# Longer planned latencies for three DMA steps in the scheduler of the second MoE

## The chip, the cores and the metric

One Trainium2 chip, one NeuronCore. The metric is the device time of one execution in microseconds (us). TensorE (PE) multiplies matrices, VectorE (DVE) and ScalarE (ACT) work elementwise, GpSimd (POOL) does little here, and SyncE (SP) issues every DMA of the part that matters. Each engine runs its own instructions in the order in which the program gives them; a later one can't pass an earlier one that still waits.

## The reference, cut to what matters

Three layers follow one another in fp32: an attention with pooled keys and values, a first MoE with ELU, and a second MoE (its weights are dense) on 4608 tokens of 512 values. Only the second is touched:

```
h = x @ w_in                                  # 4608x512 @ 512x1024
e = exp(h - max(h));  sm = e / (sum(e) + 1e-9)
solu = h * sm
ln = (solu - mean(solu)) / sqrt(var(solu) + 1e-6) * g_ln
out = ln @ w_out                              # 4608x1024 @ 1024x512
```

## The kernel before, in words

Every fp32 product is made of three products of rounded halves (high by high, low by high, high by low). So each operand has a high part, copied by ACT, and a low part, which DVE makes by subtraction.

The second MoE runs from about 877 us to the end. Its 4608 tokens are 18 pairs of tiles, each tile of 128 tokens. For pair `n` the first product is a seven-product scheme of Strassen's kind. PE makes `P1`, `P2`, `S2`, `S1`, `S3`, `T4`, `S4` (each six matmuls of 512 columns, line 1015) in three PSUM banks X, Y, Z. Between them ACT copies a bank's intermediate state to SBUF (`snap`, line 1025, tile `sn`): PE may not go on in that bank until the copy is done. After `P1`, for instance, PE makes `P2` in another bank, and then `S2` must wait for the snap of X.

The tile that becomes complete with `T4` is called A here (its values are in `hb`), the one complete with `S4` is B (in `ha`). Each then takes the same chain, with these names in the planner: `max` (DVE, line 1066), `exp` (ACT, 1072), `mul` (DVE, 1078), `sub` (ACT, 1083), `sq` (ACT, 1088), `var`. The result has to be transposed for the second product. For the 16 middle pairs, 32 tiles, that goes through DRAM: DVE transposes blocks of 32x32 (`T`, 1102), SP stores the tile to `zd` (`s`, 1107, one DMA of 512 KB), SP loads it back in four DMAs of 128 KB into `dT` (`l`, 1114). SP can't issue `l` before the store has landed. Then ACT makes the high part (`hi2`, 1122), DVE the low part (`lo2`, 1126), and PE the second product (`po`, 1153, 24 matmuls). ACT scales it into `ot` (`st`, 1159) and SP stores that to the output (1160). `os` stands for the landing of that store; the next `st` has one buffer and needs it. The first and the last pair are transposed on PE instead and have no `s` or `l`.

The order of PE's work is written out by hand (`seq`): per pair five products, `po` of B of the pair before last, `T4`, `S4`, `po` of A of the last pair. The order of ACT, DVE and SP comes from `arrange`, a list scheduler that runs when the kernel is built. Every step is an `op` with an engine, a duration, the steps that it depends on, and `lat`, the time after its end until its result may be used. From these `arrange` works out, backward, the latest start of each step at which PE's hand-written order still keeps its times, and, forward, when each becomes ready. It hands each engine the ready step with the earliest latest start, with small corrections for waits:

```python
x = min([latest[q] for q in after[k]], default=t + 3.0) - o["dur"] - o["lat"] - (gap if o["eng"] else 0.0)
latest[k] = min(x, want.get(k, x))
...
done[k] = start + o["dur"] + o["lat"]
...
(k for k in c if ready[k] <= first + look), key=lambda k: latest[k] + 3.0 * max(0.0, ready[k] - first)
```

with `gap = 0.06` and `look = 0.35`. Steps are then written to the program in the order of their planned starts. Waits in the program are set by data dependencies alone: the planned times are in no instruction.

Of the kernel before, what the change touches and what calls it, by code (L numbers as in the profile page):

```python
# [20 lines left out]
def kernel(  # L21
# [80 lines left out]
    st = {}  # L102
# [1350 lines left out]
    for pr in range(NTP):  # L1453
# [54 lines left out]
        for s in range(7):  # L1508
            banks = o_banks(s)
            for t in range(4):  # L1510
                mul_o(s, t, banks, s in (0, 1, 2), s in (1, 5, 6))
                if s + 1 < 7:
                    for i in range(2):
                        w_ring(("o", s + 1, 2 * t + i))
                    n = ORDER[s + 1]
# [47 lines left out]
    def tiles_of(n):  # L1563

        c, q = divmod(n, 2)
        return 4 * c + q + 2, 4 * c + q
# [87 lines left out]
    tiles = [i for n in range(NPAIR) for i in tiles_of(n)]  # L1654
    outs = [i for key, i in seq if key == "po"]

    def op(key, eng, dur, deps, f=None, *a, lat=0.0, at=0.0):
        ops[key] = dict(eng=eng, dur=dur, deps=deps, lat=lat, at=at, f=f, a=a)
# [3 lines left out]
    for key, n in seq:  # L1662
        k = (key, n)
        if key == "po":
            j = outs.index(n)
# [17 lines left out]
    for n, (a, b) in enumerate(map(tiles_of, range(NPAIR))):  # L1683
        if n > 1:
            c = n // 2
            if n % 2 == 0 and c > 1:
                old = [(k, 2 * c - 3) for k in ("sums", "h0", "hi", "l0", "lo")] if c > 2 else []
                op(("xl", c), "SP", 0.55, old, p2_load, c, lat=5.0, at=20.0 if c == 2 else 0.0)
            x = [("xl", c) if c > 1 else "x1", ("S4", n - 2)]
            op(("open", n), None, 0.0, x, p2_open, n)  # L1690
            op(("sums", n), "DVE", 1.45, [("open", n), ("lo", n - 2), ("hi", n - 2)], p2_sums, n)
            op(("h0", n), "ACT", 0.95, [("open", n)], p2_hi, n, slice(0, 2))
            op(("hi", n), "ACT", 1.02, [("sums", n)], p2_hi, n, slice(2, 3))
            op(("l0", n), "DVE", 1.0, [("h0", n)], p2_lo, n, slice(0, 2))
            op(("lo", n), "DVE", 1.18, [("hi", n)], p2_lo, n, slice(2, 3))
        ha = ("s" if n > 2 else "sub", B_(max(n - 2, 0)) if n > 1 else None)
        hb = ("s" if n > 2 else "mul", A_(n - 1) if n > 2 else A_(0) if n == 2 else None)
        op(("p1", n), "ACT", 0.56, [("P1", n), ("ha0", n - 1)], snap, n, "p1", "X")
        op(("u2", n), "ACT", 0.56, [("S2", n), ("hb1", n - 1)], snap, n, "u2", "X")
        op(("u3", n), "ACT", 0.56, [("S3", n), ("ha0", n), ("ha1", n - 1)], snap, n, "u3", "X")  # L1700
        op(("ha0", n), "DVE", 0.62, [("P2", n), ("p1", n), ha], z_add, n, "ha0")
        op(("hb1", n), "DVE", 0.66, [("S1", n), ("u3", n), hb], z_add, n, "hb1")
        op(("hb0", n), "ACT", 0.57, [("T4", n), ("hb1", n)], z_add, n, "hb0")
        op(("ha1", n), "DVE", 0.66, [("S4", n), ("u2", n), ("ha0", n)], z_add, n, "ha1")
        for i, h, key in ((a, ("hb0", n), "b"), (b, ("ha1", n), "a")):
            j, jo = tiles.index(i), outs.index(i)
            e2 = [(k, tiles[j - 2]) for k in ("T", "pe", "sq")] if j > 1 else []
            op(("max", i), "DVE", 1.18, [h, ("hb1", n)] + ([("st", tiles[j - 6])] if j > 5 else []), s_max, i, n, key)
            op(("exp", i), "ACT", 1.3, [("max", i)] + e2, s_exp, i)
            op(("mul", i), "DVE", 1.75, [("exp", i)], s_mul, i)  # L1710
            op(("sub", i), "ACT", 1.12, [("mul", i)], s_sub, i)
            op(("sq", i), "ACT", 1.2, [("sub", i)], s_sq, i)
            op(("var", i), "DVE", 0.12, [("sq", i)], s_var, i, lat=0.9)
            free3 = [("po", outs[jo - 3])] if jo > 2 else []
            if n in (0, last):
                op(("hi2", i), "ACT", 1.08, [("pe", i)] + free3, t_ph, i)
                op(("lo2", i), "DVE", 1.3, [("hi2", i)], t_pl, i)
            else:
                op(("T", i), "DVE", 1.18, [("sub", i)], t_dve, i)
                op(("s", i), "SP", 0.4, [("T", i)], t_store, i, lat=2.4)  # L1720
                op(("l", i), "SP", 1.75, [("s", i)] + ([("lo2", tiles[j - 2])] if n > 1 else []), t_load, i, lat=2.1)
                op(("hi2", i), "ACT", 1.0, [("l", i)] + free3, t_hi, i)
                op(("lo2", i), "DVE", 1.2, [("hi2", i)], t_lo, i)
            op(("st", i), "ACT", 0.66, [("po", i), ("var", i)] + ([("os", outs[jo - 1])] if jo else []), z_store, i)
            op(("os", i), None, 0.0, [("st", i)], lat=2.4)
    for o in ops.values():
        o["deps"] = [d for d in o["deps"] if d in ops]
    with tc.manual_schedule():
# [38 lines left out]
```

## Time and profile before

| what | value |
|---|---|
| median of three runs | 1273.57 us (1273.32 to 1275.31) |
| the profiled execution | 1271.55 us, of which its span 1269.4 us |
| granted clock of TensorE over the span | 0.993 of full speed |
| PE busy | 1242.0 us, 98% |
| DVE busy | 984.8 us, 78% |
| ACT busy | 824.0 us, 65% |
| from 870 us to the end: PE, DVE, ACT busy | 387.70, 285.60, 254.30 us |

A span runs from the first to the last instruction; a time is somewhat longer. Starts are counted from the span's start. A row of waits names the engine that stood idle and, after the arrow, what released it; PEld is PE's loading of weights, SPq the queue of SP. A granted clock of 1.00 is 2.4 GHz.

### The profile page before, as it was taken

The numbers are of one execution on the slowest core, as the hardware profiler recorded it, in microseconds if no ns is written. First come the engines' busy times: TensorE is split into PE (matmuls) and PEld (weight loads), VectorE is DVE, ScalarE is ACT, GpSimd is POOL, SyncE is SP. The second block draws the span as 40 slices with busy tenths as digits, with TensorE's granted clock in tenths as the row PEclk, the third lists the DMA queues.
The fourth block names the chain that finished last, engine by engine and source line by source line (L and its number), as shares of the span: only waits on it lengthen the run. The fifth ranks groups of instructions, "written<-read, shape, count | busy, mean of one in ns | idle before, by whom it ended". The sixth has DMA issues, their size and how long they took to land.

```text
span 1269.4 us, 17238 instructions
## 1 busy us (share of the span) xinstructions
PE 1242.0 (98%) x5768; PEld 993.9 (78%) x5768; DVE 984.8 (78%) x1484; ACT 824.0 (65%) x1405; POOL 177.7 (14%) x148
## 2 busy tenths in 40 slices
PE   8899999999999999999999999999998999999998
PEld 6777877777777878778888778888886878887777
DVE  8898687978877799676795778986886777778673
ACT  7887566666757784457764468743776667667564
POOL 4564222333210000100000000000000000000000
PEclk8999999999999999999999999999998999999999
DMA  9975366675768867787666888878454544544341
GB/s 323 296 218 191 125 220 221 214 234 168 237 205 274 252 214 243 222 294 199 203 215 201 287 254 270 288 256 306 151 172 141 158 140 143 169 147 141 108 143 57
DMA packets 177065, 263.30 MB, mean 207 GB/s; under 512 B 16465, under 2 KB 96849, under 8 KB 175953
## 3 DMA queue, kind: packets, MB, share of 16 engines
q1 hardware_dynamic: 176976, 262.21, 64.5%
q8 instruction: 46, 0.75, 0.2%
q14 instruction: 43, 0.34, 0.1%
HBM read 182.46 MB, written 79.69 MB: 207 GB/s over the span
## 4 chain that ended last, share of the span: by engine, by line
PE 64%; DVE 13%; DMA 13%; ACT 5%; issue 2%; SPq 2%; POOL 0%; ACTq 0%; DVEq 0%; POOLq 0%
PE hA L818 12%; PE oA L908 11%; PE o L694 9%; PE h L639 9%; PE po L1153 5%; DMA dT<-zd 4%; PE at L192 3%; PE oB L908 3%; PE zX L1015 3%; DMA zd<-ha 2%; PE at L277 2%; PE pt L251 2%; PE hB L818 2%; SPq L1114 2%; DVE e L1078 2%
## 5 line engine op out<-in xcount | busy, mean ns | idle before, releaser
L1153 PE MATMUL po<-w,dhl 128*128 128x512 f32 x864 | 203.7, 392 | 0.0
L908 PE MATMUL oA<-op,wr 128*128 128x512 f32 x864 | 202.4, 392 | 0.0
L908 PEld LDWEIGHTS oA<-op,wr 128*128 128x128 f32 x864 | 160.8, 188 | 38.1 <-issue 2.9
L1153 PEld LDWEIGHTS po<-w,dhl 128*128 128x128 f32 x864 | 162.1, 188 | 35.3
L898 ACT CAST op<-g 128x1024 fp32r<-128x1024 f32 x84 | 87.9, 1050 | 72.3 <-PE oA L908 33.3
L899 DVE TENSOR_TENSOR op<-g,op 128x1024 fp32r<-128x1024 f32 x84 | 102.8, 1230 | 34.1 <-ACT op L898 33.8
L818 PE MATMUL hA<-sS,wr 128*128 128x512 f32 x432 | 108.8, 394 | 1.5 <-ACT sp L830 1.5
L1015 PE MATMUL zX<-w,xh 128*128 128x512 f32 x288 | 102.8, 398 | 7.5 <-ACT sn L1025 7.4
L1093 POOL TENSOR_TENSOR sc<-sc,mhalf 128x1 f32<-128x1 f32 x36 | 21.1, 595 | 575.1 <-DVE sc L1092 300.1
L560 POOL TENSOR_TENSOR wol<-wo,woh 128x512 fp32r<-128x512 f32 x48 | 74.0, 1543 | 172.7 <-ACT woh L559 172.7
L818 PEld LDWEIGHTS hA<-sS,wr 128*128 128x128 f32 x432 | 79.9, 188 | 21.1 <-ACT sp L830 3.0
L241 POOL TENSOR_TENSOR es<-es,sm 128x720 f32<-128x720 f32 x28 | 48.2, 1720 | 305.7 <-DVE sm L239 137.3
L639 PE MATMUL h<-xh,wh 128*128 128x512 f32 x192 | 79.6, 415 | 2.4 <-DVE e L656 2.4
L694 PE MATMUL o<-gh,woh 128*128 128x512 f32 x192 | 77.5, 404 | 0.0
L838 DVE SCALAR_TENSOR_TENSOR g<-ep,g 128x512 f32<-128x512 f32 x72 | 50.9, 712 | 33.9 <-ACT ep L837 33.6
L639 PE MATMUL h<-xh,wl 128*128 128x512 f32 x192 | 76.2, 397 | 0.0
L639 PE MATMUL h<-xl,wh 128*128 128x512 f32 x192 | 76.0, 396 | 0.0
L694 PE MATMUL o<-gh,wol 128*128 128x512 f32 x192 | 75.1, 391 | 0.0
L1126 DVE TENSOR_TENSOR dhl<-dT,dhl 128x1024 fp32r<-128x1024 f32 x32 | 39.2, 1225 | 44.0 <-ACT dhl L1122 43.9
L1015 PEld LDWEIGHTS zX<-w,xh 128*128 128x128 f32 x288 | 54.7, 190 | 23.3 <-ACT sn L1025 11.0
L1122 ACT CAST dhl<-dT 128x1024 fp32r<-128x1024 f32 x32 | 33.6, 1049 | 46.9 <-DMA dT<-zd 46.8
L836 ACT ACTIVATE ep<-g 128x512 f32<-128x512 f32 x72 | 44.9, 628 | 26.2 <-DVE g L870 13.3
(354 smaller groups left out, 2759.8 us busy)
## 6 DMA issues: line engine op xcount, KB each, us to landing
wr<-w1d SPq DMA_DIRECT2D x168, 256.0 KB, 3.9
wr<-w3d SPq DMA_DIRECT2D x168, 256.0 KB, 3.0
raw<-in_w SPq DMA_DIRECT2D x48, 512.0 KB, 5.6
dT<-zd SPq DMA_DIRECT2D x128, 128.0 KB, 2.8
v<-in_v SPq DMA_DIRECT2D x32, 288.0 KB
x1r<-x1d SPq DMA_DIRECT2D x9, 1024.0 KB, 16.1
out<-ot SPq DMA_DIRECT2D x36, 256.0 KB, 3.7
w1d<-ci SPq DMA_DIRECT2D x16, 512.0 KB, 2.9
```

What stands on the lines that cost most here:

```text
L241: eng.tensor_tensor(es, es, bc(sm, n), op=ALU.mult)
L560: nc.gpsimd.tensor_tensor(ol, t[:, f % 4, :], oh.bitcast(F32), op=ALU.subtract)
L639: nc.tensor.matmul(h[:, 0:n], a[g][:, kk, fo:fo + P], x[j][:, kk, 0:n], start=(kk == 0 and m == 0), stop=(kk == KDM - 1 and m == 2), skip_ ...
L694: nc.tensor.matmul(acc, a[:, dm * P:(dm + 1) * P], x[:, 0:n], start=(f == 0 and m == 0), stop=(f == NF - 1 and m == 2))
L818: nc.tensor.matmul(bank, w[:, a, kk], x[:, b, kk], start=(start and m == 0), stop=(stop and m == 5), skip_group_check=True,)
L836: nc.scalar.activation(e, h, AF.Relu, scale=-1.0)
L838: gate["dve"] = nc.vector.scalar_tensor_tensor(d, e, 1.0, h, op0=ALU.subtract, op1=ALU.max).ins
L898: gate["act"] = nc.scalar.copy(o[:, 0], src).ins
L899: gate["dve"] = nc.vector.tensor_tensor(o[:, 1], src, o[:, 0].bitcast(F32), op=ALU.subtract).ins
L908: nc.tensor.matmul(banks[d], ws[i][:, a, d * P:(d + 1) * P], o[:, b, i], start=(start and t == 0 and i == 0 and m == 0), stop=(stop and t ...
L1015: nc.tensor.matmul(bank, x[:, o:o + P], w[:, y + k, :], start=(start and m == 0), stop=(stop and m == 5), skip_group_check=True,)
L1153: nc.tensor.matmul(po, a[:, c], b[c // 4][:, c % 4, :], start=(m == 0), stop=(m == 3 * NC2 - 1))
```

## The change

Three numbers of the plan change. The landing of the store `s` is counted at 3.0 us in place of 2.4, that of the loads `l` at 4.0 in place of 2.1, and that of the output store `os` at 3.5 in place of 2.4. No instruction is added or removed, and PE's order stays; what can differ is the order of the steps on ACT, DVE and SP (and the issue of POOL's small steps, which go with `var`).

```diff
                 op(("T", i), "DVE", 1.18, [("sub", i)], t_dve, i)
-                op(("s", i), "SP", 0.4, [("T", i)], t_store, i, lat=2.4)
-                op(("l", i), "SP", 1.75, [("s", i)] + ([("lo2", tiles[j - 2])] if n > 1 else []), t_load, i, lat=2.1)
+                op(("s", i), "SP", 0.4, [("T", i)], t_store, i, lat=3.0)
+                op(("l", i), "SP", 1.75, [("s", i)] + ([("lo2", tiles[j - 2])] if n > 1 else []), t_load, i, lat=4.0)
                 op(("hi2", i), "ACT", 1.0, [("l", i)] + free3, t_hi, i)
                 op(("lo2", i), "DVE", 1.2, [("hi2", i)], t_lo, i)
             op(("st", i), "ACT", 0.66, [("po", i), ("var", i)] + ([("os", outs[jo - 1])] if jo else []), z_store, i)
-            op(("os", i), None, 0.0, [("st", i)], lat=2.4)
+            op(("os", i), None, 0.0, [("st", i)], lat=3.5)
```

## Rows read from the trace of the kernel before

**Rows 1.** Waits of PE's matmuls, 870 us on: waiter, releaser, total us, times, longest.

```profile
PE zX L1015 <- ACT sn L1025: 7.4, 6, 4.1
```

**Rows 2.** Busy time of a stretch: length, then PE, PEld, DVE, ACT, POOL, clock, DMA.

```profile
960.00:980.00 20.00, 15.88 (x59) 12.44 (x58) 13.09 (x26) 12.04 (x19) 1.61 (x3) 0.83 0.62 183
```

**Rows 3.** Waits of all engines, 870 us on.

```profile
ACT dhl L1122 <- DMA dT<-zd: 46.8, 28, 4.2
```

**Rows 4.** Timeline of ACT around 970 us: start, length, idle before with its releaser.

```profile
969.69 1.04 ACT L1122 CAST dhl<-dT 128x1024 fp32r<-128x1024 f32 x1 [4.17 <-DMA dT<-zd]
970.64 1.14 ACT L1083 ACTIVATE e<-e,sc 128x1024 f32<-128x1024 f32 x1
971.82 1.06 ACT L1088 ACTIVATE sq<-e 128x1024 bf16<-128x1024 f32 x1
...
972.88 0.57 ACT L1025 COPY sn<-zX 128x512 f32<-128x512 f32 x1
```

**Rows 5.** Timeline of PE at the same place.

```profile
973.50 0.79 PE L1015 MATMUL zX<-w,xh 128*128 128x512 f32 x1 [4.12 <-ACT sn L1025]
```

**Rows 6.** Chain of waits that ended last, its pieces there: start, us, what.

```profile
973.50 2.93 PE zX L1015 x6
976.42 2.56 PE zZ L1015 x6
978.98 1.39 PE zX L1015 x6
980.37 5.49 PE po L1153 x24
```

**Rows 7.** Timelines of DVE and SP: the tile of rows 4, its transposition and DMAs.

```profile
958.76 1.24 DVE L1102 STREAM_TRANSPOSE ha<-e 128x1024 f32<-128x1024 f32 x1
...
960.02 0.38 SPq L1107 DMA_DIRECT2D zd<-ha  x1
960.46 0.54 SPq L958 DMA_DIRECT2D x1r<-x1d  x1
963.29 1.74 SPq L1114 DMA_DIRECT2D dT<-zd  x4
```

**Rows 8.** Timelines of DVE, SP and ACT: `T`, `s`, `hi2` of the tile with the longest way.

```profile
1189.54 1.24 DVE L1102 STREAM_TRANSPOSE ha<-e 128x1024 f32<-128x1024 f32 x1
...
1192.84 1.27 SPq L1107 DMA_DIRECT2D zd<-ha  x1
...
1201.38 1.05 ACT L1122 CAST dhl<-dT 128x1024 fp32r<-128x1024 f32 x1 [2.56 <-DMA dT<-zd]
```

**Rows 9.** Query of the tile `dT`, 880 us on: issue to landing of one quarter.

```profile
DMA to landing us min/median/max: 2.2/2.8/5.3
```

**Rows 10.** Timelines of DVE and PE: `T`, `lo2`, `po` of the first tile A.

```profile
907.20 1.23 DVE L1102 STREAM_TRANSPOSE hb<-e 128x1024 f32<-128x1024 f32 x1
...
916.75 1.22 DVE L1126 TENSOR_TENSOR dhl<-dT,dhl 128x1024 fp32r<-128x1024 f32 x1 [0.62 <-ACT dhl L1122]
...
919.58 0.62 PE L1153 MATMUL po<-w,dhl 128*128 128x512 f32 x2
```

**Rows 11.** The same three for the tightest tile A, the fourteenth of sixteen.

```profile
1186.88 1.23 DVE L1102 STREAM_TRANSPOSE hb<-e 128x1024 f32<-128x1024 f32 x1
...
1197.07 1.23 DVE L1126 TENSOR_TENSOR dhl<-dT,dhl 128x1024 fp32r<-128x1024 f32 x1 [2.51 <-ACT dhl L1122]
...
1199.39 0.85 PE L1153 MATMUL po<-w,dhl 128*128 128x512 f32 x3
```

**Rows 12.** The same three for the last tile A.

```profile
1226.50 1.25 DVE L1102 STREAM_TRANSPOSE hb<-e 128x1024 f32<-128x1024 f32 x1
...
1235.98 1.22 DVE L1126 TENSOR_TENSOR dhl<-dT,dhl 128x1024 fp32r<-128x1024 f32 x1 [1.17 <-ACT dhl L1122]
...
1241.51 0.85 PE L1153 MATMUL po<-w,dhl 128*128 128x512 f32 x3
```

**Rows 13.** Waits of SP's queue, 880 us on.

```profile
SPq L1160 <- ACT ot L1159: 100.8, 30, 10.7
```

## The prediction

> **What bounds the kernel now.** The page says that PE is busy for 98% of the span, so a gain can come only from the little that PE loses. Which part of that lies in the second MoE is read from the waits of PE from 870 us on: six waits of 7.4 us in sum, all of them for a snap (line 1025) [rows 1]. The longest is 4.1 us. The busy time by stretch shows that it cost more than its length: from 960 to 980 us the granted clock is 0.83 [rows 2], so part of that stretch ran at 1.2 GHz. The chain of waits gives the size: the two products behind the gap took 2.93 and 2.56 us, the next one 1.39 [rows 6], so (2.93 - 1.39) + (2.56 - 1.39) = 2.7 us. PE's loss here that any order could give back is 7.4 + 2.7 = 10.1 us.
>
> Next, why a snap is late. At the long gap, PE's wait in bank X ended at 973.50 with a snap [rows 5] that ACT began only at 972.88 [rows 4]. In front of it ACT stood idle for 4.17 us with `hi2` at its head, waiting for a load, and then ran `hi2`, `sub` and `sq` before the snap. Nothing of these three is needed by `S2`. And the tile was in no hurry: `hi2` ended at 970.73 and `lo2` takes 1.22 us [rows 10], so it was ready near 972.0, while its `po` began at 980.37 [rows 6]. It is a tile B. All six gaps have this form: a `hi2` of a tile B that waited between 1.5 and 4.2 us and then a late snap; the first is that of rows 4, the last that of rows 8.
>
> The waits of all engines say how common the cause is: ACT waited for the loads at 28 of 32 `hi2`, 46.8 us in sum [rows 3]. Mostly PE had enough in hand; six times not.
>
> **Why the plan puts `hi2` too early.** From the end of `T` to the earliest `hi2` the old plan counts 0.06 + 0.4 + 2.4 + 0.06 + 1.75 + 2.1 + 0.06 = 6.83 us, so 6.83 + 1.0 + 0.06 = 7.89 to the earliest `lo2`. In the trace, `lo2` begins 8.3 us after the end of `T` for the first tile A, 9.0 for the fourteenth, 8.2 for the last [rows 10 to 12]. For the B of rows 4, `hi2` began 9.69 us after `T` ended at 960.00 [rows 4, 7]; a load of x went out on the same queue between its store and its loads [rows 7]. The longest way of all 32 is 1201.38 - 1190.78 = 10.60 us [rows 8]. So the old plan is too short nearly always, by 0.1 to 3.8 us, and ACT meets `hi2` before its data.
>
> **The change, part by part.** Nothing is added or removed; the work of each engine stays. Two things happen in the planner.
>
> First, `hi2` can't be planned before 6.83 + (3.0 - 2.4) + (4.0 - 2.1) = 9.33 us after `T`. In ACT's order it moves behind what becomes ready in those 2.5 us: at the gap of rows 4 that is `sub` (1.14 us), `sq` (1.06) and the snap (0.57), which is the right cure. ACT will then wait only for loads that take longer. Of the 32, six did so, by 3.3 us in sum; the longest is 10.60 - 9.33 = 1.27 us [rows 8], the B of rows 4 has 9.69 - 9.33 = 0.36. So of 46.8 us of waiting some 3.3 remain. What remains of PE's gaps lies between nothing and these 3.3; four of the six are among the tiles for which a wait remains. Gaps have been shorter than the waits behind them (7.4 against 46.8 in all, 4.12 against 4.17 at worst), so I take 0.8. The clock's loss goes with the long gap. This term is 10.1 - 0.8 = 9.3 us of gain, between 0 (other steps come to stand in front of the snaps in the same way) and 10.1.
>
> Second, all that leads to `T` becomes due 2.5 us earlier, and tiles A lose room. From the end of `T` to the start of `po` they had 11.15, 11.28 and 13.76 us in rows 10, 11 and 12; 11.15 is the least and 12.97 the mean of the sixteen. The new plan wants 9.33 + 1.0 + 0.06 + 1.2 = 11.59. If `T` stays where it is, three of sixteen miss that, by 0.4, 0.3 and less than 0.1 us: 0.8 us of PE waiting for `lo2`. If moreover one more step of 1.15 us falls in front of `hi2` or `lo2`, the need is 12.74, seven of sixteen miss it, and the sum is 6.3 us. If `T` is planned earlier, as its earlier due time makes likely where DVE has a choice, the loss is nothing. I take 0.8, the value without any further accident, and keep 0 and 6.3.
>
> An earlier due time for A has its own price: `max`, `exp`, `mul` and `sub` of A now win against other steps more often, and on ACT these are the snaps. A snap takes 0.57 us [rows 4] and PE has 1.39 us of work in the other bank [rows 6]: 0.8 us to spare. An `exp` or `sub` of 1.15 us begun just before a snap is ready holds PE for 0.35 us; `sub` and `sq` together, 2.4 us with the accumulator's read, for 1.6. The trace of before has such a queue only behind a wait, so the bounds are 0 and, once in each of 16 pairs at the higher price, 26. The planner compares due times and a snap's is within 0.8 us of its ready time, while A keeps some of its room; so I take three cases at 0.35, about 1.0 us.
>
> B's room is no concern (8.4 us in the case above, and 2.5 are taken). The landing of `os` matters to `st` alone: outputs come 8.2 or more us apart (`po`, 5.49, with 2.7 us of products between), and 0.66 + 3.5 is less, so this edit costs nothing; at the end, with two `po` in a row, 5.49 still covers it. On SP, `l` is planned 0.6 us later and may fall behind an output store, whose wait for `st` is up to 10.7 us [rows 13]. Today's case of this kind is the 2.0 us for which the `s` of rows 8 was held, behind loads that waited for their own store. The plan's later `l` lets such an `s` go ahead and may hold another `l`; I set both against each other, at nothing, with 2.0 us of a tile's room as the bound, which B's room covers.
>
> Sum: -9.3 + 0.8 + 1.0 = -7.5 us. The profiled execution took 1271.55 us, so it would take 1264.05; the median of the runs is 2.0 us higher, and the gain taken from it gives 1266.1.
>
> The Trainium skill says otherwise (DMA: Bandwidth & Descriptors, Anatomy of one DMA): it counts about 2.0 us and the bytes at 436 GB/s, which makes an estimate of 2.3 us for a quarter of 128 KB. That is for DMAs issued by GpSimd; by it the old 2.1 is about right, the new 4.0 is 1.7 us too long, and the tiles are held back for nothing. The trace's median is 2.8, its longest 5.3 [rows 9].
>
> **The rivals.** *The plan now holds back tiles whose data is there.* Typical A tiles had `lo2` 8.2 to 9.0 us after `T` and the plan now says 10.39, so 1.4 to 2.2 us are given away. For it: A's least room. Against it: even then only three miss. With one more step in front, PE loses 6.3 us at `po`, the gain is 9.3 - 6.3 = 3.0, and the time 1270.5. It cancels the gain where the delay beyond the plan reaches 1.5 us. The rule of the skill above is this rival's.
>
> *Nothing changes on PE.* The wait for loads goes, but ACT then stands before another step in the new order, the snaps are as late as now, and the time is 1273.6. For it: the order is a list order that minds ACT's other waits no better than before. Against it: the six gaps have one cause.
>
> *A's steps get in front of the snaps; the kernel becomes slower.* At 0.9 us for each of 16 pairs, between 0.35 and 1.6, PE loses 14.4 us against 8.5 gained otherwise: 1279.5 us. It decides from 8.5 / 16 = 0.53 us a pair on. For it: the due time of `exp` moves by 2.5 us. Against it: the planner's own PE would be late by this, which its due times are made to avoid.
>
> **How the numbers follow.** The forecast has 0.62, with a range of its own from 1262.5 to 1269.5; the first rival 0.17, the second 0.09, the slower one 0.12. About 0.2%, 2.5 us, is what a measurement of this kernel can tell from no change. The first rival's 3.0 us lie close to that: 0.10 of its 0.17 count as faster, 0.07 as the same. So faster 0.72, same 0.07 + 0.09 = 0.16, slower 0.12. The range goes from 1262.5, where all 10.1 us and a little of the runs' surplus come back, to 1273.6, which takes in the first two rivals and leaves out the slower one and little else.
>
> **What would show it.** Right: ACT's wait for `dT` falls from 46.8 us to under 10; PE's waits for snaps to under 2; the clock is 1.00 all through the stage; at most a few waits of `po` for `lo2` (line 1126), under 0.5 us each. Wrong: waits of `po` for DVE at many tiles A; or PE's waits for snaps stay, with `exp`, `sub` or `sq` in front of the snap on ACT and no wait for a load before them. A gain that is missing while ACT's wait for the loads is gone would break the claim that this wait is the cause.

## The result, and the profile after

The changed kernel takes 1261.05 us (median of four runs, 1260.74 to 1261.29) against 1274.17 us of the kernel before on the same chip (four runs, 1273.32 to 1275.31): a ratio of 0.9896, 95% interval 0.9879 to 0.9913. It is faster by 13.1 us, which is more than the forecast's 7.5, and its median lies 1.45 us below the low end of the range. (The forecast had three of the four runs of before, with a median of 1273.57.) The profiled execution took 1260.74 us, its span is 1259.0 us.

The waits of the loading of weights, from 870 us on, are the shortest way to see what happened. First the kernel before, which had this row beside those of [rows 1]:

```profile
PEld zX L1015 <- ACT sn L1025: 11.0, 9, 4.6
```

The changed kernel has one short wait left, at the start of the second MoE, and its matmuls have none at all:

```profile
PEld zX L1015 <- DVE xl L996: 0.5, 1, 0.5
```

ACT's waits in the changed kernel, same view:

```profile
ACT sn L1025 <- PE zX L1015: 45.4, 46, 2.3
...
ACT dhl L1122 <- DMA dT<-zd: 3.1, 3, 1.9
```

The second row answers to [rows 3]: 46.8 us of waiting for loads have become 3.1. The first shows what took their place: ACT now stands ready at the snaps and waits for PE, 45.4 us in place of 25.8. The stretch of [rows 2] again, in the changed kernel (length, busy of PE, PEld, DVE, ACT, POOL, clock, DMA):

```profile
960.00:980.00 20.00, 20.00 (x89) 16.34 (x88) 16.55 (x32) 13.83 (x20) 1.96 (x4) 1.00 0.54 172
```

The clock stays at 2.4 GHz there. The tile of [rows 4, 7], the third B, on DVE, SP and ACT in the changed kernel:

```profile
956.46 1.25 DVE L1102 STREAM_TRANSPOSE ha<-e 128x1024 f32<-128x1024 f32 x1 [0.60 <-ACT e L1083]
...
957.74 0.38 SPq L1107 DMA_DIRECT2D zd<-ha  x1
...
960.53 1.74 SPq L1114 DMA_DIRECT2D dT<-zd  x4
...
962.38 0.54 SPq L958 DMA_DIRECT2D x1r<-x1d  x1
...
967.43 1.03 ACT L1122 CAST dhl<-dT 128x1024 fp32r<-128x1024 f32 x1
```

`hi2` begins 9.7 us after the end of `T` (957.71 us), as late as in [rows 4], but ACT has worked up to it and the data is there. The load of x, too, has moved from ahead of the four loads to behind them.

The tile of [rows 11], the fourteenth A, in the changed kernel (DVE and PE: `T`, `lo2`, `po`):

```profile
1174.21 1.25 DVE L1102 STREAM_TRANSPOSE hb<-e 128x1024 f32<-128x1024 f32 x1 [1.22 <-ACT e L1083]
...
1185.41 1.18 DVE L1126 TENSOR_TENSOR dhl<-dT,dhl 128x1024 fp32r<-128x1024 f32 x1
...
1189.74 0.39 PE L1153 MATMUL po<-w,dhl 128*128 128x512 f32 x1
```

From the end of `T` to `po` it has 14.28 us; it had 11.28. `lo2` ends 3.15 us before `po` begins, and no `po` waits anywhere.

### The profile page after: what moved, and what is told of

Its sections match the earlier page's. It is cut to its first block, busy times and chain, and to the rows that moved or that the text cites. A ratio compares the mean times of both kernels' runs of the same rounds, so it can differ in the third digit from the quotient of the medians.

```text
span 1259.0 us, 17236 instructions
## 1 busy us (share of the span) xinstructions
PE 1235.2 (98%) x5768; PEld 990.1 (79%) x5768; DVE 985.9 (78%) x1484; ACT 822.3 (65%) x1405; POOL 178.6 (14%) x148
## 4 chain that ended last, share of the span: by engine, by line
PE 85%; DVE 6%; DMA 5%; ACT 2%; issue 1%; SPq 1%; POOL 0%; ACTq 0%; DVEq 0%; POOLq 0%
PE po L1153 16%; PE hA L818 12%; PE oA L908 12%; PE h L639 10%; PE o L694 9%; PE zX L1015 8%; PE zZ L1015 4%; PE at L192 3%; PE oB L908 3%; PE at L277 2%; PE pt L251 2%; PE zY L1015 2%; PE hB L818 2%; DMA w2d<-cv 1%; DMA raw<-in_w 1%
## 5 line engine op out<-in xcount | busy, mean ns | idle before, releaser
L836 ACT ACTIVATE ep<-g 128x512 f32<-128x512 f32 x72 | 44.8, 628 | 25.9 <-DVE g L870 13.3
L1025 ACT COPY sn<-zX 128x512 f32<-128x512 f32 x54 | 31.7, 587 | 45.7 <-PE zX L1015 45.4
L892 DVE TENSOR_TENSOR g<-g,g 128x1024 f32<-128x1024 f32 x48 | 61.3, 1290 | 0.1
```

Of the source, the lines that this page charges most:

```text
L892: nc.vector.tensor_tensor(d, x, y, op=op)
```

## The experiments

All times of one run and its kernel before are from one chip; chips differ (the kernel before has medians from 1271.18 to 1274.17 us), so the ratios are to be compared. "ACT" is ACT's wait for the loads, "PEld" the waits of the loading of weights for a snap (or for `lo2`, where it says so), both in us from 870 us on. "hi2" is the planned distance from the end of `T`, worked out as in the prediction. "po" is the time from the start of the first matmul of a `po` to the start of the last in the profiled execution, in us: PE has the same work in this stretch in every run, so what a run has above 355.1 is PE's loss there.

| kernel | hi2 | ACT | PEld | po | median | ratio (95%) |
|---|---|---|---|---|---|---|
| before | 6.83 | 46.8 | 11.0 | 367.0 | | 1 |
| changed | 9.33 | 3.1 | 0 | 355.1 | 1261.05 | 0.9896 (0.9879 to 0.9913) |
| e1 loads 4.0 | 8.73 | 8.2 | 0.7 | 355.1 | 1260.44 | 0.9909 (0.989 to 0.9927) |
| e2 store 3.0 | 7.43 | 38.4 | 8.6 | 362.3 | 1266.76 | 0.9964 (0.9951 to 0.9977) |
| e3 output store 3.5 | 6.83 | 52.9 | 16.5 | 375.4 | 1281.54 | 1.0074 (1.0053 to 1.0095) |
| e4 before, loads don't wait | 6.83 | 25.9 | 4.4 | 358.6 | 1264.34 | 0.9939 (0.9922 to 0.9957) |
| e5 forward pass only | 9.33 | 10.1 | 0.7 (`lo2`) | 355.7 | 1261.13 | 0.9917 (0.9898 to 0.9936) |
| e6 due times only | 6.83 | 40.0 | 10.0 | 365.4 | 1269.43 | 0.9979 (0.9968 to 0.9991) |
| e7 tiles B only | 9.33 for B | 28.2 | 5.8, 0.7 (`lo2`) | 362.3 | 1266.11 | 0.9957 (0.9941 to 0.9973) |
| e8 changed, output store 2.4 | 9.33 | 5.2 | 0 | 355.1 | 1260.40 | 0.9910 (0.989 to 0.993) |
| e9 changed, longer still | 12.33 | 0 | 10.0 (`lo2`) | 363.6 | 1268.05 | 0.9958 (0.9944 to 0.9973) |
| e10 medians 2.9, 2.8 | 8.03 | 16.4 | 1.6 | 355.5 | 1262.51 | 0.9915 (0.9897 to 0.9933) |
| e11 e3, loads don't wait | 6.83 | 22.2 | 8.1 | 365.7 | 1270.12 | 0.9983 (0.9969 to 0.9997) |
| e12 tiles A only | 9.33 for A | 10.1 | 0.5 | 355.4 | 1261.16 | 0.9904 (0.9888 to 0.992) |
| e13 e3, x load behind | 6.83 | 45.1 | 10.6 | 365.8 | 1274.54 | 1.0023 (1.0003 to 1.0042) |
| e14 before, x load behind | 6.83 | 42.4 | 11.0 | 365.8 | 1271.34 | 0.9996 (0.9976 to 1.0016) |

**e1, the loads alone.**

```diff
-                op(("l", i), ..., t_load, i, lat=2.1)
+                op(("l", i), ..., t_load, i, lat=4.0)
```

> Kernel before with the loads alone counted at 4.0 us (store 2.4, output store 2.4 as before): hi2 is planned 8.73 us after T. Theory 1 (ACT stood at hi2 before its load had landed, so a snap behind it came late and PE waited): most loads have landed by then, ACT waits under 10 us for them in place of 46.8, PE's waits for snaps fall from 7.4 to under 1.5, time 1261 to 1265 us. Theory 2 (any other order of ACT and DVE moves the time by several us either way; the change was lucky): no tie between the wait for loads and the time.

Ratio 0.9909, ACT's wait 8.2 us, PE without waits but at the start. This is as theory 1 had it. This one number gives the whole gain, within the intervals.

**e2, the store alone.**

```diff
-                op(("s", i), "SP", 0.4, [("T", i)], t_store, i, lat=2.4)
+                op(("s", i), "SP", 0.4, [("T", i)], t_store, i, lat=3.0)
```

> Kernel before with the store to DRAM alone counted at 3.0 us: hi2 is planned 7.43 us after T, near the quickest loads. Theory 1: ACT still waits for many loads, some 25 to 35 us in sum, and PE keeps about half of its loss; 1266 to 1272 us. Theory 2: no tie.

The result lies between: 38.4 us of ACT's wait, somewhat more than expected, and a third of the gain. PE's longest gap here, 2.6 us, is of another kind. ACT stood for 3.1 us at an output copy (`st`), until the output store before it had landed, and the snap came behind that copy. SP had issued that store 0.6 us after a load of x.

**e3, the output store alone.**

```diff
-            op(("os", i), None, 0.0, [("st", i)], lat=2.4)
+            op(("os", i), None, 0.0, [("st", i)], lat=3.5)
```

> Kernel before with the output store alone counted at 3.5 us: hi2 stays planned 6.83 us after T. Theory 1: ACT's wait for loads stays at 40 us or more, PE's loss stays, 1271 to 1277 us. Theory 2: another order and so another time, several us off.

Here the expectation of theory 1 failed and that of theory 2, another time by several us, came true: 0.7% slower, with ACT's wait at 52.9 us. A number that names nothing of the transposed tiles moved the time by 10 us. The trace shows that theory 1's mechanism is at work here too. SP and then ACT and PE at ACT's longest wait:

```profile
1001.05 0.38 SPq L1107 DMA_DIRECT2D zd<-ha  x1
1001.47 0.54 SPq L958 DMA_DIRECT2D x1r<-x1d  x1
...
1004.23 1.78 SPq L1114 DMA_DIRECT2D dT<-zd  x4
...
1011.46 1.04 ACT L1122 CAST dhl<-dT 128x1024 fp32r<-128x1024 f32 x1 [5.37 <-DMA dT<-zd]
...
1015.84 0.80 PE L1015 MATMUL zX<-w,xh 128*128 128x512 f32 x1 [4.12 <-ACT sn L1025]
```

It is the picture of [rows 4, 5, 7] again: a load of x of 1 MB (and here an output store, not shown) goes out between a tile's store and its loads, the loads land late, `hi2` holds ACT, and the snap is late for PE. In this order it happens at three tiles, with waits of 4.6 to 5.4 us.

**e4, the order of before with loads that don't wait for their store.** From the second pair on, a tile loads what the pair before stored, so the second product is made from another tile.

```diff
-                in_=zd[i % 4][x].rearrange("(r f) e -> f r e", r=4),
+                in_=zd[i % 4 if i in (1, 3) else (i % 4) ^ 1][x].rearrange("(r f) e -> f r e", r=4),
```

> Kernel before, its order untouched, but from the second pair on the loads of a transposed tile read the DRAM tile that the pair before stored (so the second product is made from the wrong tile), and need not wait for their own store to land: dT is there some 2.8 us earlier. Theory 1: ACT's wait for loads is nearly gone without any change of order, PE's waits for snaps with it, 1260 to 1265 us. If the gain came from the new order itself (steps of tile A planned earlier, or luck), the time stays at 1272 to 1276 us.

Without any change of order ACT's wait falls to 25.9 us, PE's to 4.4, and more than half of the gain appears (0.9939). The wait for the loads is thus a cause and not a companion. It isn't gone. Of the 20 waits left, the three longest (2.2 to 3.2 us) stand behind loads that SP issued 0.6 us after a load of x; the others were not traced to a cause.

**e5 and e6, the forward pass alone and the due times alone.**

```diff
-            done[k] = start + o["dur"] + o["lat"]
+            done[k] = start + o["dur"] + {"s": 3.0, "l": 4.0, "os": 3.5}.get(k[0] if isinstance(k, tuple) else k, o["lat"])
```

> The three new latencies count only in the planner's forward pass (when a result may be used); its due times keep the old ones. So hi2 is planned 9.33 us after T, but nothing before T becomes due earlier. Theory 1 (the place of hi2 behind other steps of ACT is what counts): ACT's wait for loads under 10 us, PE without waits, 10 to 13 us under the time of before. Theory 3 (tiles A got their steps planned earlier, and that made the room): most of the gain is gone, and PE waits at po of tiles A for lo2.

```diff
-            x = min([latest[q] for q in after[k]], default=t + 3.0) - o["dur"] - o["lat"] - (gap if o["eng"] else 0.0)
+            x = min([latest[q] for q in after[k]], default=t + 3.0) - o["dur"] - {"s": 3.0, "l": 4.0, "os": 3.5}.get(k[0] if isinstance(k, tuple) else k, o["lat"]) - (gap if o["eng"] else 0.0)
```

> The three new latencies count only in the planner's due times; the forward pass keeps the old ones, so the chain of each tile is due 2.5 us earlier but hi2 stays planned 6.83 us after T. Theory 1: ACT still waits 35 to 55 us for loads, PE keeps waits for snaps, the time within 5 us of before, to either side. Theory 3: most of the gain is here, 8 us or more.

The gain is in the forward pass (0.9917), as theory 1 says: it is the later place of `hi2`. The due times alone bring 0.2%, so theory 3 falls.

**e7 and e12, tiles B alone and tiles A alone.** Store and loads get the new numbers for one kind (`key` is "a" for tiles B, "b" for tiles A); the output store stays at 2.4.

```diff
-                op(("s", i), ..., t_store, i, lat=2.4)
-                op(("l", i), ..., t_load, i, lat=2.1)
+                op(("s", i), ..., t_store, i, lat=3.0 if key == "a" else 2.4)
+                op(("l", i), ..., t_load, i, lat=4.0 if key == "a" else 2.1)
```

> The new latencies of store and loads for tiles B alone; tiles A and the output store keep the old ones. All six waits of PE in the kernel before stood behind a hi2 of a tile B. Theory 1 in its narrow form (it was the B tiles): 8 to 13 us under before, with ACT's wait left at tiles A only, 15 to 25 us in sum. Theory 1 in its wide form (any hi2 met too early costs, and which tile PE feels is chance): about half the gain, 4 to 8 us.

> The new latencies of store and loads for tiles A alone; the counterpart of the run for tiles B (ratio 0.9957, ACT's wait 28 us). Theory 1 in its wide form: half of the waits remain, 20 to 30 us, and 3 to 7 us are gained. In its narrow form (B tiles matter): nothing is gained, 3 us to either side.

This went against the narrow form altogether, and e12 went beyond the wide one, which had expected 3 to 7 us. All six gaps of the kernel before stood behind a `hi2` of a tile B, yet the numbers for B alone give less than half of the gain, and those for A alone give all of it (0.9904), with B's own `hi2` still planned at 6.83 us. In e12 ACT waits for loads 11 times, 1.6 us at most. B's `hi2` began 6.8 to 10.2 us after the end of `T` there, half of them at 8.8 or later, so in this order it came later than its own numbers ask; why was not worked out. In e7 ACT's longest wait, 5.7 us, stood at a tile A. So the tile at the head of a gap need not be the one to change.

**e8, the changed kernel with the output store back at 2.4.**

```diff
-            op(("os", i), None, 0.0, [("st", i)], lat=3.5)
+            op(("os", i), None, 0.0, [("st", i)], lat=2.4)
```

> The changed kernel with the output store back at 2.4 us: store 3.0 and loads 4.0 remain. Alone, 3.5 us for the output store made the kernel slower by 0.7%. Theory 1: that came through earlier meetings of hi2 with its load in another order; with hi2 planned late enough there is nothing to meet, so the time is that of the changed kernel within 3 us, 10 to 13 us under before. Theory 2 (each order has its own luck): the output store's latency moves the time by several us here too.

The ratio is 0.9910, inside the interval of the changed kernel. The third edit is worth nothing where `hi2` has room, and it costs 10 us where it has none (e3). Theory 2, by which it should move the time by several us here too, falls.

**e9, longer still.**

```diff
-                op(("s", i), ..., t_store, i, lat=3.0)
-                op(("l", i), ..., t_load, i, lat=4.0)
+                op(("s", i), ..., t_store, i, lat=4.0)
+                op(("l", i), ..., t_load, i, lat=6.0)
```

> The changed kernel with store 4.0 and loads 6.0 us in place of 3.0 and 4.0: hi2 is planned 12.33 us after T, and with hi2 and lo2 the plan wants 14.59 us from T to po, where tiles A of the changed kernel have 14.3 in its regular stretch. Theory 1 with its other side (the first rival of the prediction, tiles held back whose data is there): ACT waits for no load, but PE waits at po of tiles A for lo2, 0.3 to 1 us each, so 3 to 12 us slower than the changed kernel, 0 to 9 under before. Theory 4 (the longer the better): the time of the changed kernel, 10 to 13 us under before.

More than half of the gain is lost again. ACT waits for no load at all, and PE waits for `lo2`, once at each of the 16 tiles A. The waits of the loading of weights in e9:

```profile
PEld po L1153 <- DVE dhl L1126: 10.0, 16, 0.7
```

One of these places on ACT and PE, by time:

```profile
1022.23 0.68 ACT L1159 ACTIVATE ot<-po,sc 128x512 f32<-128x512 f32 x1
1022.81 1.03 ACT L1122 CAST dhl<-dT 128x1024 fp32r<-128x1024 f32 x1
...
1024.50 0.40 PE L1153 MATMUL po<-w,dhl 128*128 128x512 f32 x1
1025.16 0.73 PE L1153 MATMUL po<-w,dhl 128*128 128x512 f32 x2 [0.26 <-DVE dhl L1126]
```

This is the prediction's first rival, at a latency beyond the one chosen: the output copy stands in front of `hi2`, and `po` begins on the high part and waits for the low.

**e10, the medians of the trace.**

```diff
-                op(("s", i), ..., t_store, i, lat=2.4)
-                op(("l", i), ..., t_load, i, lat=2.1)
+                op(("s", i), ..., t_store, i, lat=2.9)
+                op(("l", i), ..., t_load, i, lat=2.8)
```

> Kernel before with store 2.9 and loads 2.8 us, the medians of the trace, output store as before: hi2 is planned 8.03 us after T. Theory 1: about half of the loads land later than that, so ACT waits 10 to 25 us and the time is 5 to 9 us under before, short of the 11 that the loads alone at 4.0 gave (hi2 at 8.73). If the medians are enough for the plan, the gain is the full 10 to 13.

ACT's wait is 16.4 us as expected, but the gain is the full one within the intervals (0.9915): of the waits that remain, little reaches PE. Of PEld's 1.6 us, 0.9 stand at the start of the second MoE, where no transposed tile is loaded yet.

**e11, the order of e3 with loads that don't wait for their store** (the edits of e3 and e4 together).

> The order of the kernel with the output store alone at 3.5 us (10 us slower than before), with loads that read the tile of the pair before and need not wait for their own store (so the second product is made from the wrong tile). Theory 1 (that order too is slow through waits for loads): ACT's wait falls from 52.9 to about 25 us, and the time to 5 to 9 us under before. Theory 2 (the order itself is bad, by other waits): it stays 3 to 10 us slower than before.

The ratio falls by 0.0091, from 1.0074 to 0.9983. That is less than theory 1 expected and more than theory 2 did. Its longest wait, 5.3 us, stands again behind a load of x that SP issued 1.4 us ahead of the tile's loads. That the order of e3 is bad by itself isn't excluded by this run; e13 says more.

**e13 and e14, the load of x behind the tile's loads**, in the order of e3 and in that of before. ACT's and DVE's orders stay.

```diff
-        for k in arrange(ops, seq, {"PE": 0.0, "ACT": 0.3, "DVE": 4.0, "SP": 0.0}):
+        plan = arrange(ops, seq, {"PE": 0.0, "ACT": 0.3, "DVE": 4.0, "SP": 0.0})
+        for c in range(3, NPAIR // 2):
+            at = plan.index(("xl", c))
+            to = next(n for n in range(at, len(plan)) if plan[n][0] == "l" or plan[n] == ("open", 2 * c))
+            assert plan[to][0] == "l"
+            plan.insert(to, plan.pop(at))
+        for k in plan:
```

> The kernel with the output store alone at 3.5 us (ratio 1.0074), its order of ACT and DVE untouched; on SP six loads of x are issued right behind the loads of the next transposed tile in place of ahead of them. If the load of x is what makes these loads late: the three waits of 4.6 to 5.4 us shrink to 1.5 to 2.5, ACT's wait falls from 52.9 to 40 us or so, PE's two gaps of 4 us go, and the time falls to that of before or up to 6 us under it. If the order of ACT is to blame: still 5 to 10 us above before.

> The kernel before, its order of ACT and DVE untouched, with the same move of six loads of x on SP. If the load of x is what makes loads late: the wait of 4.17 us falls to about 1.5, PE's gap of 4.12 us and the 2.7 us of half clock go, other gaps stay as waits of hi2 remain at nearly all tiles; 4 to 8 us under before. If not: within 2 us of before.

In e13 the three long waits shrink to 2.0 to 2.8 us and the loss falls from 0.74% to 0.23%: the loads of x caused most of it. But the time doesn't reach that of before, as was expected, and ACT's wait is 45.1 us and not 40: a new wait of 6.1 us, the longest of that run, stands behind a store that SP issued 0.6 us after a load of x, and PE has a new gap of 4.1 us later on. In e14 the wait of 4.17 us shrinks to 1.59, as expected, but the time, expected 4 to 8 us lower, doesn't move (0.9996). A new long wait stands elsewhere here too. SP and ACT of e14 there:

```profile
1063.05 0.54 SPq L958 DMA_DIRECT2D x1r<-x1d  x1
1064.92 0.39 SPq L1107 DMA_DIRECT2D zd<-ha  x1
1071.68 1.74 SPq L1114 DMA_DIRECT2D dT<-zd  x4
...
1075.90 1.05 ACT L1122 CAST dhl<-dT 128x1024 fp32r<-128x1024 f32 x1 [4.55 <-DMA dT<-zd]
```

Now the next tile's store falls behind the load of x, and the loads wait 6.8 us for it to land. So a load of x in front of a tile's loads (e3), of its store (e13, e14) or of an output store (e2) held ACT; moving it moved the wait. In these runs only room in the order took the wait away.

## Why the prediction was wrong

Its mechanism was right: `hi2` was planned ahead of its data, ACT stood at it, a snap came late and PE waited; e1, e4 and e5 show it, and all signs that the prediction gave for being right came. That ACT's remaining wait was forecast at 3.3 us and is 3.1 is luck: of the forecast's six tiles, five of them B, only one still waits, 0.2 us; the rest stands at the last two tiles A, where ACT reached `hi2` earlier after `T` than planned. The sign and the cause hold, and the size failed. The step is the last sum, "-9.3 + 0.8 + 1.0 = -7.5 us", with what stands ahead of and behind it:

- *Costs that didn't come, 2.6 us.* The forecast left 0.8 us of PE's gaps in place, 0.8 for `po` of tiles A and 1.0 for steps of A in front of snaps. All three are nothing in the changed kernel. Tiles A lost no room: from the end of `T` to `po` the mean rose from 12.97 to 14.00 us, and the tightest tile of [rows 11] gained 3 us. The least, 11.15 us at the first tile A, stayed as it was, and `lo2` ended there 0.5 us before `po`. The due times alone (e6) give this room too, a mean of 14.13 us; in the forward pass alone (e5) it is 13.56, and PE waited for `lo2` once, 0.7 us.
- *A loss that wasn't counted, 1.8 us.* From the first `po` of a tile A (919.58 us before, 921.08 after) to the end, the profiles differ by 1269.4 - 1259.0 + 1.5 = 11.9 us, and the forecast knew 10.1. A wait of PE is counted from the end of a matmul, and a row gives a matmul 0.39 us, while undisturbed ones start 0.23 us apart. So a gap costs more by the starts of the matmuls than by its wait. PE in the kernel before, at its second gap:

```profile
1037.91 0.40 PE L1015 MATMUL zY<-w,xh 128*128 128x512 f32 x1
1038.95 0.50 PE L1015 MATMUL zX<-w,xh 128*128 128x512 f32 x1 [0.65 <-ACT sn L1025]
1039.29 0.40 PE L1015 MATMUL zX<-w,xl 128*128 128x512 f32 x1
```

The two steps from start to start take 1.04 and 0.34 us in place of 0.23 each: 0.92 us lost, where the wait says 0.65. By this reading 0.27 to 0.29 us go uncounted at each of the five gaps at full clock, 1.4 us in all. Two more waits of PEld, 0.24 and 0.52 us at 1017.36 and 1122.43 us, show no wait in the rows of the matmuls and cost 0.07 and 0.36 us by the starts. That makes the 1.8 us.
- *The runs, 2.3 us.* The forecast took the gain from the median and let the 2.0 us stay by which the runs were above the profiled execution. Before, the median of all four runs is 1274.17 - 1271.55 = 2.6 us above it, after, 1261.05 - 1260.74 = 0.3. Whether this is loss given back or the chance of one profiled execution is open: in the experiments the median lay between 2.5 us under the profiled execution (e4) and 4.7 above it (e13).

Against these, the changed kernel's profile begins the stage 1.5 us later, in work that is the same, and its time lies 0.4 us closer to its span: -7.5 - 2.6 - 1.8 + 1.5 - 0.4 - 2.3 = -13.1 us.

Of the single steps: that the output store's latency costs nothing holds in the changed kernel (e8) and fails alone (e3), as the step looked at its own wait only and not at what a new order does to the other two. In e2 an output copy began 5.85 us after the issue of the output store before it, which it had waited for; the step had allowed 3.5. That 4.0 us is too long for the loads was the other reading: 2.8 is enough (e10) and 6.0, with 4.0 for the store, is too long (e9), but 4.0 costs nothing, as tiles A had the room. The rule of the Trainium skill that the prediction weighed (DMA: Bandwidth & Descriptors, Anatomy of one DMA), with its estimate of 2.3 us for a quarter, speaks for the shorter latency; the trace of before has a median of 2.8 [rows 9], and that the longer latency holds tiles back for nothing didn't show in the time. The reading of the tile B as the one to move was wrong (e7, e12). The first rival is real and begins somewhere between 9.33 and 12.33 us. The slower rival did not appear: in the changed kernel, e5 and e8 no snap kept PE waiting, in e1 only one at the start of the second MoE, for 0.3 us.

## What to carry to other kernels

In an order fixed at build time, count a latency that varies at what it reaches under load, up to the room of its consumer. A wait planned too short holds all that stands behind it on the same engine, and in an order without room a small edit can cost several us (e3: 0.7% by a number that had nothing to do with it); too long costs only from the point where the consumer's own user waits (e9).

The waits of an in-order engine for DMAs say where to look, but not what the cure is worth. ACT's wait of 22.2 us goes with a ratio of 0.9983 (e11), one of 25.9 with 0.9939 (e4) and one of 28.2 with 0.9957 (e7). The worth is read from the starts of the bounding engine's own work: by the column "po" of the table the kernel before loses 11.9 us of PE's time, where the waits of the matmuls showed 7.4, and the changed kernel, e1 and e8 end at the same 355.1.

## What the runs showed that was not expected

One load of 1 MB, issued 1.2 to 2.9 us ahead, made the four loads of a tile begin to be used 5.8 to 7.2 us after their issue in place of about 4.1 (three tiles each of before and e3), and one issued 0.6 to 1.9 us ahead of a store put 7.2 and 6.8 us between that store and the loads that wait for it, in place of 2.8 (e13, e14). And what a gap of PE costs is not told by its length alone: the granted clock fell to half, 1.2 GHz, after waits of 4.1 us (before), 3.5 (e7) and 1.9 (e6, e14), and stayed at 2.4 GHz after waits of 2.5 (e14) and 2.6 (e2, e6). What decides between them no run here shows.
